# Splitting the channel product of an attention and spectral-mixing kernel into two products made under the weight stream, with a tail of four matmuls per tile

## The chip, the cores and the metric

The kernel runs on one core of one Trainium2 chip. The metric is device time in microseconds (us) of one launch. Three runs of the kernel before took 563.3, 560.01 and 556.01 us, median 560.01 us. The profile is of one further execution, which took 558.66 us; the span between its first and its last instruction is 556.9 us.

A core has a matrix engine (PE, with its weight loads shown apart as PEld), a vector engine (DVE), a scalar engine (ACT), a general engine (POOL) and a sync engine (SP). POOL, SP and ACT can issue DMA copies, which all run on the core's same 16 DMA engines. Products land in PSUM; DVE and ACT move them to SBUF.

## The reference

```python
scores = scale * np.matmul(q, k.transpose(0, 1, 3, 2))     # 8 batches, 8 heads, 576 positions, 64 wide
mask = (rel >= 0) & (rel < 64)                             # causal window of 64
attn = softmax(where(mask, scores, -1e9))
x = heads of matmul(attn, v) joined                        # (8, 576, 512)

X = np.fft.rfft(x, axis=1)                                 # 64 lowest modes are mixed
Yr = einsum('bmd,mde->bme', Xr, w_r) - einsum('bmd,mde->bme', Xi, w_i)
Yi = einsum('bmd,mde->bme', Xr, w_i) + einsum('bmd,mde->bme', Xi, w_r)
y = np.fft.irfft(Y, n=S, axis=1)
u = x + y
out = u + np.maximum(u @ w_ch, 0.0)
```

The mode weights `w_r` and `w_i` are 64 matrices of 512x512 each in float32: 134 MB to read. The output is 9.44 MB of float32. The channel product is `u @ w_ch`, with one 512x512 matrix for all positions.

## The kernel before, in words

**Weights.** POOL's queue carries the weights: 256 copies of 256 KB (as written; each reads 512 KB of float32 and casts to bf16), one per mode, half of the input channels, and real or imaginary part (`load_weights`, L94 to L106). A tile is 128 partitions by 1024 elements. The first 8 tiles go to the pool `wave`, the others to `ring` with 25 buffers, and after the attention to a second ring of 24 more. POOL issues in order, each copy waits on its engine's queue until its buffer is free, and until the copy eight places earlier has landed (eight semaphores are shared in turn).

**Attention.** A hand-written software pipeline (L379 to L410) runs over 40 units of heads and positions. It leaves the attention output `x_sb` in bf16 and its forward transform `XQ` for both channel halves. After half of the units it also runs ten early steps (`early_step`): one per group of four modes, with the first channel half; their sums wait in `Yacc`.

**The stream.** Then 22 late steps follow (L441 to L448). `mode_step` does 16 matmuls on eight weight tiles: 32 output rows per mode, four modes side by side in the array. Groups 10 to 15 take two steps each (both halves), then groups 0 to 9 one each. `finish_group` moves a finished group from PSUM to the SBUF tile `stg` on DVE (L425 or L427) and issues eight copies of 8 KB from SP's queue (L430, L431). Each takes 8 rows of `stg` (one per batch, 1 KB each) to one partition of `Yall`, where the mode stands on the partition and the batch in the row:

```python
nc.sync.dma_start(out=late["Yall"][m:m + 1, :, :], in_=stg[r0:r0 + B, :])
```

**The seam.** When the stream is done, the table `trigI` of the inverse transform is made (L454 to L474: an iota on POOL, then DVE, a sine on ACT, then DVE). DVE has the last three `stg` behind this in its order.

**The tail.** For each of 40 tiles (8 batches, 4 tiles of 128 positions and one of 64) PE does one matmul for the inverse transform (L488), DVE adds `x_sb` (L491), PE transposes the sum in float32 four times (L494), ACT or DVE moves that to SBUF (L498), PE does four matmuls with `wch` (L501), DVE takes the maximum with zero and adds (L505), and SP issues the store (L507).

The order within each engine is as written inside `manual_schedule`; the seam and the tail stand outside of it and are interleaved by the planner.

Of the kernel before, what the change touches and what calls it, by code (L numbers as in the profile page):

```python
# [17 lines left out]
RING = 25  # L18
# [7 lines left out]
def kernel(  # L26
# [40 lines left out]
    mask_t = consts.tile([128, 3, 4, 128], BF16, name="mask_t")  # L67
    trigF = consts.tile([128, NTC, 2 * NM], BF16, name="trigF")
    trigI = consts.tile([2 * NM, S], BF16, name="trigI")
# [9 lines left out]

    ring = pool("ring", bufs=RING, side="right")  # L80
    wave = pool("wave", bufs=FIRST, side="right")
# [3 lines left out]
    order = [(p, 0) for p in range(4 * EARLY)]  # L85
    for grp in range(EARLY, NGRP):
        order += [(4 * grp + i, hb) for hb in range(2) for i in range(4)]
    for grp in range(EARLY):
        order += [(p, 1) for p in range(4 * grp, 4 * grp + 4)]
    wlist = [(p, hb, ri) for p, hb in order for ri in range(2)]  # L90
    wtiles = {}
    nload = 0

    def load_weights(n):  # L94
        nonlocal nload
        for _ in range(n):
            if nload == len(wlist):
                return
            p, hb, ri = wlist[nload]
            w = (wave if nload < FIRST else ring).tile(  # L100
                [128, NJ, DM], BF16, name="wi" if ri else "wr", tag="wt")
            src = moe_w_i if ri else moe_w_r
            nc.gpsimd.dma_start(  # L103
                out=w, in_=src[p, HALF * hb:HALF * hb + HALF, :].rearrange("(p j) e -> p j e", j=NJ))
            wtiles[p, hb, ri] = w
            nload += 1  # L106


    def mode_step(psm, pairs, hb, first, last):
# [10 lines left out]
        for p in pairs:  # L120
            for ri in range(2):
                wtiles.pop((p, hb, ri))

    with tc.manual_schedule():
        ps_mm = pool("ps_mm", space=PSUM)
        rawp = pool("rawp", bufs=2)
# [191 lines left out]
        zero_xq(0, nc.vector)  # L318

# [40 lines left out]
        def early_step():  # L360
            nonlocal step, post
            grp = step
            late["psm"] = ps_mm.tile([128, DM], FP32, name="psm")
            psm = late["psm"]
            mode_step(psm, range(4 * grp, 4 * grp + 4), 0, first=True, last=True)
            load_weights(8 if step >= FIRST // 8 else 0)
            if step == FIRST // 8 - 1:
                close(wave)
                post = pool("post", side="right", reuse_waits="tile")
                XQ[1] = post.tile([128, NJ, NM + 1, 3, B], BF16, name="XQ1")  # L370
                zero_xq(1, nc.gpsimd)
                late["Yacc"] = post.tile([128, EARLY, DM], FP32, name="Yacc")
                late["Yall"] = post.tile([2 * NM, B, DM], BF16, name="Yall")
            nc.scalar.copy(out=late["Yacc"][:, grp, :], in_=psm)
            step += 1

        post = None

        for it in range(-3, NU + 3):  # L379
# [24 lines left out]
            if 0 <= it < NA:  # L404
                load_weights((it + 1) * (FIRST + RING) // NA - nload)
# [3 lines left out]
            if it >= NA and (it - NA) % 2 == 0 and step < EARLY:  # L409
                early_step()  # L410
        do_dft(NG - 1)
# [3 lines left out]
        close(smp, ptp, pp, ps_m, ps_pv, ps_pt, ps_s, vdp, vfp, qtp, rawp, ps_mm)  # L415

        ring2 = pool("ring2", bufs=24, reuse_waits="tile")
        stgpool = pool("stgpool", bufs=3, reuse_waits="tile")
        ps_mc = pool("ps_mc", bufs=3, space=PSUM, reuse_waits="tile")
        nc.gpsimd.dma_start(out=wch, in_=moe_w_ch.rearrange("(c p) e -> p c e", p=128))  # L420

        def finish_group(grp, psm):
            stg = stgpool.tile([128, DM], BF16, name="stg")
            if grp < EARLY:
                nc.vector.tensor_tensor(out=stg, in0=psm, in1=late["Yacc"][:, grp, :], op=ALU.add)  # L425
            else:
                nc.vector.tensor_copy(out=stg, in_=psm)  # L427
            for g in range(4):
                m, r0 = 4 * grp + g, 32 * g
                nc.sync.dma_start(out=late["Yall"][m:m + 1, :, :], in_=stg[r0:r0 + B, :])  # L430
                nc.sync.dma_start(out=late["Yall"][NM + m:NM + m + 1, :, :], in_=stg[r0 + B:r0 + 2 * B, :])  # L431

        ring_, ring = ring, ring2
        load_weights(24)
        late_steps = []
        for grp in range(EARLY, NGRP):
            late_steps += [(grp, 0, True, False), (grp, 1, False, True)]
        for grp in range(EARLY):
            late_steps.append((grp, 1, True, True))
        psm = None  # L440
        for grp, hb, f, l in late_steps:  # L441
            if f:
                psm = ps_mc.tile([128, DM], FP32, name="psm")
            mode_step(psm, range(4 * grp, 4 * grp + 4), hb, f, l)
            ring = ring_ if nload % 16 < 8 else ring2
            load_weights(8)
            if l:
                finish_group(grp, psm)  # L448

    close(ps_mc, stgpool, ring2)  # L450

    with ExitStack() as p15:
        stmp2 = p15.enter_context(tc.tile_pool(name="stmp2", bufs=1))
        MtI = stmp2.tile([128, S], FP32, name="MtI")  # L454
        nc.gpsimd.iota(MtI, pattern=[[1, S]], base=0, channel_multiplier=0,
                       allow_small_or_imprecise_dtypes=True)
        nc.vector.tensor_scalar(out=MtI, in0=MtI, scalar1=Mcol, scalar2=None, op0=ALU.mult)
        Gph = stmp2.tile([128, 1], FP32, name="Gph")
        nc.vector.tensor_scalar(out=Gph, in0=Gcol, scalar1=0.25, scalar2=0.25, op0=ALU.mult, op1=ALU.add)
        Qi = stmp2.tile([128, S], FP32, name="Qi")  # L460
        Ri = stmp2.tile([128, S], FP32, name="Ri")
        nc.vector.tensor_scalar(out=Qi, in0=MtI, scalar1=1.0 / S, scalar2=Gph, op0=ALU.mult, op1=ALU.add)
# [77 lines left out]
```

## Time and profile before

| what | value |
|---|---|
| median of three runs | 560.01 us |
| profiled execution, its span | 558.66 us, 556.9 us |
| PE busy, PEld busy, DVE busy, ACT busy | 323.2, 181.5, 188.0, 137.3 us |
| last weight matmuls begin | 454.65 us into the span |
| first matmul of the tail | 481.32 us |
| last store's DVE instruction begins | 553.01 us |
| weight copies, median issue to landing | 9.7 and 9.8 us |
| bytes moved by POOL's queue | 77.63 MB as written |

The page divides the span into 40 slices and gives each engine's busy tenths, the clock granted to PE in tenths, and the busy share of the DMA engines. The chain is the sequence of work that ended last, followed back from the end. A timeline row gives start, duration, engine, line, operation, tiles and count, and in brackets how long the engine was idle before it and what ended that. A DMA answer gives packets by size and by queue, in the window asked for; q0 is POOL's queue, q1 the queues of SP and ACT. The share beside a queue is the time of its packets over 16 engines.

### The profile page before, as it was taken

What the parts mean: (1) busy time and instruction counts of PE and PEld (TensorE: products, weight loads), DVE (VectorE), ACT (ScalarE), POOL (GpSimd) and SP (SyncE); (2) the same over time, 40 slices, a digit from 0 to 9 for tenths busy, and PEclk for the clock granted to TensorE, in tenths of its full rate; (3) what the DMA queues carried; (4) which work ended last, traced back from release to release, by engine and by line L of the source; (5) the groups of instructions that cost most, each with busy time, mean ns of one, the idle gap of its engine ahead of it and who ended that gap; (6) DMA issues with size and microseconds to landing.
All of it is one profiled execution on the core that took longest, in us unless ns stands there. A gap on an engine that the chain in (4) does not pass through costs nothing.

```text
span 556.9 us, 9561 instructions
## 1 busy us (share of the span) xinstructions
PE 323.2 (58%) x3868; PEld 181.5 (33%) x3896; DVE 188.0 (34%) x329; ACT 137.3 (25%) x216; POOL 217.9 (39%) x356
## 2 busy tenths in 40 slices
PE   0598889797884696442343343433433420499996
PEld 0466666665653463100000000000000000266664
DVE  6267366465560364000000000000000022288885
ACT  0455564656651545100000000000000001022221
POOL 7184574654743636443444344344344400000000
PEclk9999696789995889655555555555555555599999
DMA  9799999999899998999999999999999940034343
GB/s 156 117 160 192 193 203 199 181 163 184 144 206 203 203 208 158 209 209 247 210 210 211 211 209 211 210 211 211 211 205 211 210 87 8 8 141 138 136 136 130
DMA packets 95676, 98.17 MB, mean 176 GB/s; under 512 B 47504, under 2 KB 57744, under 8 KB 95632
## 3 DMA queue, kind: packets, MB, share of 16 engines
q0 software_dynamic: 50192, 77.63, 77.4%
q1 hardware_dynamic: 45440, 19.93, 15.5%
q8 instruction: 30, 0.49, 0.3%
q14 instruction: 14, 0.11, 0.1%
HBM read 163.58 MB, written 9.44 MB: 311 GB/s over the span
## 4 chain that ended last, share of the span: by engine, by line
DMA 49%; PE 28%; ACT 7%; issue 5%; SPq 4%; DVE 4%; POOL 2%; POOLq 0%; DVEq 0%; ACTq 0%
DMA wi<-in_moe_w_i_dram 33%; DMA vf<-in_v_dram 9%; DMA wr<-in_moe_w_r_dram 7%; PE pout L501 7%; PE tr L169 3%; PE psut L494 3%; PE s L219 3%; PE pt L227 2%; PE psy L488 2%; ACT XQ L270 2%; PE s L193 2%; PE s L204 2%; ACT p L221 2%; PE px L268 1%; SPq L151 1%
## 5 line engine op out<-in xcount | busy, mean ns | idle before, releaser
L115 PE MATMUL psm<-wr,XQ 128*32 128x512 bf16 x256 | 68.9, 545 | 142.5 <-DMA wr<-in_moe_w_r_dram 141.9
L103 POOL DMA_DIRECT2D wi<-in_moe_w_i_dram x128 | 68.8, 538 | 78.6 <-DMA wi<-in_moe_w_i_dram 60.2
L103 POOL DMA_DIRECT2D wr<-in_moe_w_r_dram x128 | 68.8, 538 | 76.5 <-DMA wr<-in_moe_w_r_dram 67.4
L115 PEld LDWEIGHTS <-XQ 128*32 128x32 bf16 x512 | 19.3, 104 | 220.9 <-issue 204.0
L211 DVE TENSOR_REDUCE mx<-s 128x4 fp32r<-128x512 f32 x72 | 49.8, 691 | 75.1 <-PE s L201 64.1
L469 ACT ACT_TABLE_LOAD x1 | 1.3, 1283 | 230.0 <-DVE Qi L467 230.0
L427 DVE CAST stg<-psm 128x512 bf16<-128x512 f32 x6 | 4.1, 691 | 130.1 <-PE psm L115 130.1
L115 PE MATMUL psm<-wi,XQ 128*32 128x512 bf16 x256 | 43.8, 557 | 6.5 <-DMA wi<-in_moe_w_i_dram 6.5
L501 PE MATMUL pout<-wch,utt 128*128 128x512 f32 (+1 forms) x160 | 43.6, 410 | 0.5 <-ACT utt L498 0.5
L221 ACT ACTIVATE p<-s 128x512 bf16<-128x512 f32 x72 | 40.2, 606 | 9.4 <-PE s L219 8.4
L498 ACT CAST utt<-psut 128x512 fp32r<-128x512 f32 (+1 forms) x33 | 19.1, 579 | 70.3 <-PE psut L494 70.3
L169 PE MATMUL tr<-ident_bf,rawk 72*64 72x72 bf16 x512 | 17.5, 219 | 31.4 <-DMA rawk<-in_k_dram 21.1
L491 DVE TENSOR_TENSOR ut<-x_sb,psy 128x512 f32<-128x512 bf16 (+1 forms) x40 | 27.1, 683 | 18.7 <-PE psy L488 17.2
L505 DVE SCALAR_TENSOR_TENSOR ot<-pout,ut 128x512 f32<-128x512 f32 (+1 forms) x40 | 27.5, 687 | 14.4 <-PE pout L501 14.4
L230 DVE COPY pts<-pt 128x1024 bf16<-128x1024 bf16 (+1 forms) x40 | 25.3, 633 | 19.0 <-PE pt L227 19.0
L172 ACT COPY kT<-tr 128x576 bf16<-128x576 bf16 x32 | 20.4, 638 | 44.1 <-PE tr L169 44.1
L219 PE MATMUL s<-mx,ident_r 128*128 128x512 f32 x72 | 30.6, 497 | 0.1
L425 DVE TENSOR_TENSOR stg<-psm,Yacc 128x512 bf16<-128x512 f32 x10 | 6.7, 689 | 68.4 <-PE psm L115 39.5
L501 PEld LDWEIGHTS pout<-wch,utt 128*128 128x128 f32 (+1 forms) x160 | 26.3, 177 | 10.5 <-ACT utt L498 3.2
L204 PE MATMUL s<-kT,qT 64*64 64x64 bf16 x320 | 26.5, 212 | 4.9 <-issue 4.9
L258 DVE TENSOR_TENSOR x_sb<-o,r 128x512 bf16<-128x512 f32 (+1 forms) x40 | 27.6, 690 | 1.4
L488 PE MATMUL psy<-Yall,trigI 128*128 128x512 bf16 (+1 forms) x34 | 12.3, 401 | 26.0 <-DMA Yall<-stg 25.7
(85 smaller groups left out, 510.4 us busy)
## 6 DMA issues: line engine op xcount, KB each, us to landing
wr<-in_moe_w_r_dram POOLq DMA_DIRECT2D x128, 256.0 KB, 9.7
wi<-in_moe_w_i_dram POOLq DMA_DIRECT2D x128, 256.0 KB, 9.8
vf<-in_v_dram SPq DMA_DIRECT2D x64, 128.0 KB
out_dram<-ot SPq DMA_DIRECT2D x32, 256.0 KB
rawk<-in_k_dram POOLq DMA_DIRECT2D x16, 288.0 KB, 7.9
rawq<-in_q_dram POOLq DMA_DIRECT2D x16, 288.0 KB, 8.6
Yall<-stg SPq DMA_DIRECT2D x128, 8.0 KB
vf<-in_v_dram SPq DMA_DIRECT2D x16, 64.0 KB
```

The source lines that it names most:

```text
L103: nc.gpsimd.dma_start(out=w, in_=src[p, HALF * hb:HALF * hb + HALF, :].rearrange("(p j) e -> p j e", j=NJ))
L115: nc.tensor.matmul(out=psm[32 * g:32 * g + 32, :], lhsT=XQ[hb][:, j].rearrange("k m t b -> k (m t b)")[:, (3 * p + 1 - ri) * B:(3 * p + 5 ...
L169: nc.tensor.transpose(out=pt[64 * hh:64 * hh + 64, j, :], in_=raw[:, 2 * pr + hh, j, :], identity=ident_bf[0:72, 0:72])
L204: nc.tensor.matmul(out=s[ro, t, 0:64], lhsT=lq, rhs=kT[ro, 64 * n:64 * n + 64], start=False, stop=True, skip_group_check=True)
L211: nc.vector.tensor_reduce(out=mx, in_=s, axis=AX.X, op=ALU.max, negate=True)
L219: nc.tensor.matmul(out=s, lhsT=ident_r, rhs=mx.unsqueeze(2).to_broadcast([128, 4, 128]), start=False, stop=True, skip_group_check=True)
L221: nc.scalar.activation(out=p[:, 4 * c2:4 * c2 + 4, :], in_=s, func=ACT_F.Exp, scale=EX_SCALE)
L230: nc.vector.tensor_copy(out=ps[:, 0:nt, :], in_=pt[:, 0:nt, :])
L258: nc.vector.tensor_tensor(out=xo.rearrange("p c (h d) -> p c h d", d=64), in0=ov[:, :, :, 0:64], in1=rb, op=ALU.mult)
L491: nc.vector.tensor_tensor(out=ut[:nt, :], in0=x_sb[:nt, b, tch, :], in1=psy[:nt, :], op=ALU.add)
L501: nc.tensor.matmul(out=pout[:nt, :], lhsT=utt[:, ech * nt:(ech + 1) * nt], rhs=wch[:, ech, :], start=(ech == 0), stop=(ech == NDCH - 1))
L505: nc.vector.scalar_tensor_tensor(out=ot[:nt, :], in0=pout[:nt, :], scalar=0.0, in1=ut[:nt, :], op0=ALU.max, op1=ALU.add)
```

## The change

`u @ w_ch` becomes `x @ w_ch` plus `y @ w_ch`, and the second is the inverse transform of `Y @ w_ch`. Both new factors are made during the stream:

- `x_product` makes `XW`, 40 tiles of `x @ w_ch`, two after each late step (sixteen in the first eight of the first ten steps, two after each of the last twelve). `finish_group` also makes `Z = Y @ w_ch` for the group's four modes. Both use `channel_product`: four bf16 transposes on PE, a copy on ACT, four float32 matmuls on PE.
- The result of a group goes to `Yall` in four copies of 16 KB instead of eight of 8 KB, and to `Zall` (float32) in four copies of 32 KB. Each takes 16 rows of the staging tile to two partitions; mode rows are now interleaved (real, imaginary). All are issued by SP, except the last group's `Zall` copies, which ACT issues.
- The inverse tables (`trigI`, and a float32 one, `trigIr`) are made before the first late step. Their iota stands in POOL's queue behind the loads of the early steps.
- The tail has four matmuls per tile: identity times `x_sb` and the inverse transform of `Yall` into one bank, identity times `XW` and the inverse transform of `Zall` into another; then a copy on ACT, a maximum and sum on DVE and the store.
- The weight tiles of a step come real parts first, then imaginary (before: alternating). The order of steps is groups 0 to 9 (second half), then 10 to 15. The rings are 11 and 14 buffers and no second ring of 24; once the weights of the first ten late steps are in, only the ring of 11 is used, and `XW` takes the other's place. `wch` is loaded after the sixth early step rather than after the attention.

```diff
-    ring = pool("ring", bufs=RING, side="right")
+    ringA = pool("ringA", bufs=NRA, side="right", reuse_waits="tile")
+    ringB = pool("ringB", bufs=NRB, side="right", reuse_waits="tile")
...
+    steps = [(grp, 0) for grp in range(EARLY)] + [(grp, 1) for grp in range(EARLY)]
+    steps += [(grp, hb) for grp in range(EARLY, NGRP) for hb in range(2)]
+    wlist = [(p, hb, ri) for grp, hb in steps for ri in range(2) for p in range(4 * grp, 4 * grp + 4)]
...
+        def channel_product(src, n):
+            pt = ps_t.tile([128, NDCH, 128], BF16, name="ptr")
+            for c in range(NDCH):
+                nc.tensor.transpose(out=pt[:, c, 0:n], in_=src[0:n, 128 * c:128 * c + 128],
+                                    identity=ident_bf[0:n, 0:n])
+            tr = trpool.tile([128, NDCH, 128], FP32R, name="tr")
+            nc.scalar.copy(out=tr[:, :, 0:n], in_=pt[:, :, 0:n])
+            pz = ps_z.tile([128, DM], FP32, name="pz")
+            for c in range(NDCH):
+                nc.tensor.matmul(out=pz[0:n, :], lhsT=tr[:, c, 0:n], rhs=wch[:, c, :],
+                                 start=(c == 0), stop=(c == NDCH - 1))
+            return pz
...
         def finish_group(grp, psm):
...
-            for g in range(4):
-                m, r0 = 4 * grp + g, 32 * g
-                nc.sync.dma_start(out=late["Yall"][m:m + 1, :, :], in_=stg[r0:r0 + B, :])
-                nc.sync.dma_start(out=late["Yall"][NM + m:NM + m + 1, :, :], in_=stg[r0 + B:r0 + 2 * B, :])
+            pz = channel_product(stg, 128)
+            zst = stgpool.tile([128, DM], FP32R, name="zst")
+            nc.vector.tensor_copy(out=zst, in_=pz)
+            last = grp == NGRP - 1
+            for t, rows, eng in ((Yall, stg, nc.sync),
+                                 (Zall.bitcast(FP32), zst.bitcast(FP32), nc.scalar if last else nc.sync)):
+                for g in range(4):
+                    m2, r0 = 2 * (4 * grp + g), 32 * g
+                    eng.dma_start(out=t[m2:m2 + 2, :, :], in_=rows[r0:r0 + 2 * B, :])
...
+        def x_product(n):
+            for _ in range(n):
...
+                pz = channel_product(x_sb[:, b, c, :], rows[i])
+                xw = late["xp"].tile([128, DM], FP32R, name=f"xw{i}")
+                nc.vector.tensor_copy(out=xw[0:rows[i]], in_=pz[0:rows[i]])
+                XW[i] = xw
...
+        inverse_tables()
...
+        for i, (grp, hb) in enumerate(steps[EARLY:]):
...
+            mode_step(psm, range(4 * grp, 4 * grp + 4), hb, f, hb == 1)
+            load_weights(len(wlist))
+            if hb == 1:
+                finish_group(grp, psm)
+            if i < EARLY:
+                x_product(min(2, NX0 - len(XW)))
+            else:
...
+                x_product(2)
...
+        for i, (b, c) in enumerate(tiles):
...
+            nc.tensor.matmul(out=psu[:nt, :], lhsT=ident_bf[:nt, :nt], rhs=x_sb[:nt, b, c, :], start=True, stop=False)
+            nc.tensor.matmul(out=psu[:nt, :], lhsT=trigI[:, ts_], rhs=Yall[:, b, :], start=False, stop=True)
...
+            nc.tensor.matmul(out=pso[:nt, :], lhsT=ident_r[:nt, :nt], rhs=XW[i][:nt, :], start=True, stop=False)
+            nc.tensor.matmul(out=pso[:nt, :], lhsT=trigIr[:, ts_], rhs=Zall[:, b, :], start=False, stop=True)
+            ut = ringA.tile([128, DM], FP32, name="ut", tag="wt")
+            nc.scalar.copy(out=ut[:nt, :], in_=psu[:nt, :])
+            nc.vector.scalar_tensor_tensor(out=ut[:nt, :], in0=pso[:nt, :], scalar=0.0,
+                                           in1=ut[:nt, :], op0=ALU.max, op1=ALU.add)
+            nc.sync.dma_start(out=out[b, 128 * c:128 * c + nt, :], in_=ut[:nt, :])
```

## The prediction

> **What bounds the kernel now.** I read the slices of the page first, then the chain of waits, the timeline around the end of the weights, and the DMA answers for three windows. The slices, four of their rows:
>
> ```profile
> PE   0598889797884696442343343433433420499996
> ...
> DVE  6267366465560364000000000000000022288885
> ...
> PEclk9999696789995889655555555555555555599999
> DMA  9799999999899998999999999999999940034343
> ```
>
> A slice is 13.9 us. From slice 17 to 32 the DMA engines are full, PE is busy 4 tenths at half clock and DVE does nothing: the late steps wait for weights. Then come two slices in which nothing is busy (the seam), then the tail, where PE is full. The last late steps, the seam and the tail, from the timeline and the chain:
>
> ```profile
> 246.31 1.01 PE L115 MATMUL psm<-wi,XQ 128*32 128x512 bf16 x5 [0.27 <-DMA wi<-in_moe_w_i_dram]
> 256.32 1.01 PE L115 MATMUL psm<-wi,XQ 128*32 128x512 bf16 x5 [0.27 <-DMA wi<-in_moe_w_i_dram]
> 268.87 1.01 PE L115 MATMUL psm<-wi,XQ 128*32 128x512 bf16 x5 [0.17 <-DMA wi<-in_moe_w_i_dram]
> 278.89 1.01 PE L115 MATMUL psm<-wi,XQ 128*32 128x512 bf16 x5 [0.17 <-DMA wi<-in_moe_w_i_dram]
> ...
> 434.60 1.01 PE L115 MATMUL psm<-wi,XQ 128*32 128x512 bf16 x5 [0.31 <-DMA wi<-in_moe_w_i_dram]
> 444.63 1.01 PE L115 MATMUL psm<-wi,XQ 128*32 128x512 bf16 x5 [0.19 <-DMA wi<-in_moe_w_i_dram]
> ```
>
> ```profile
> 463.42 0.69 DVE stg L425
> ...
> 479.27 1.92 DMA Yall<-stg
> 481.32 0.58 PE psy L488
> ...
> 553.01 0.68 DVE ot L505
> ```
>
> A step of eight tiles takes 10.02 us where nothing else moves (246.31 to 256.32, 434.60 to 444.63), 1.25 us per tile. The one step with `wch` in it takes 12.55 us: 1 MB, 32 rows of 2 KB on each of 16 engines, cost 2.53 us, 79 ns per row. So other bytes are not free: they lengthen the stream. From 278.89 to 434.60 there are 15 steps, 150.3 us at 10.02, but 155.7 pass: 5.4 us for the 11 groups whose `Yall` copies fall in it, 0.49 us per group. The DMA answers, first for 456 to 482 us (only `Yall` copies), then for 485 to 556 us (only stores):
>
> ```profile
> DMA packets 385, 0.21 MB, mean 8 GB/s; under 512 B 192, under 2 KB 384, under 8 KB 384
> q1 hardware_dynamic: 384, 0.20, 3.7%
> ```
>
> ```profile
> DMA packets 5252, 9.49 MB, mean 134 GB/s; under 512 B 640, under 2 KB 640, under 8 KB 5248
> q1 hardware_dynamic: 5248, 9.44, 38.4%
> ```
>
> 40 stores leave 640 tiny packets, 16 each: one end mark per DMA engine. 24 `Yall` copies leave 192, 8 each: a copy of 8 rows runs on 8 engines, a row (1 KB) and a mark on each. Engine time: 3.7% of 16 x 26 us over 192 pairs is 80 ns for row and mark; 38.4% of 16 x 71 us over 4608 rows and 640 marks is 91 ns per 2 KB row if a mark is 25 ns (estimate; at 0 to 40 ns the row is 95 to 89). And 0.49 us per group over eight copies is 61 ns per pair: the eight engines were the same in all eight copies (spread evenly over 16 it would be 4 pairs, 122 ns each, more than their 80), and the tile of weights waits for its slowest engine.
>
> **Part 1, the seam.** Before: last weight matmuls end at 455.27 (454.65 + 0.62), the tail starts at 481.32. Gone are 7 us of tables and 24 copies at 0.68 us each. What takes their place, in a chain at half clock: `stg` on DVE 0.9 (0.69 and the hand-over); four transposes 0.7 (eight bf16 ones take 0.97 at full clock, L227); ACT 0.7 (0.59); four products 1.9 (1.00 at full clock, L501); `zst` 0.8; four `Zall` copies on ACT at SP's 0.68, 2.7. Behind these in ACT's queue stand the copies of the last two `x_product`, on which PE waits before the tail: 0.6, then products 1.5, transposes 0.6, copy 0.7, products 1.5. Sum 12.6 us. The last `Zall` copy lands 1.92 us after its issue (the chain's row for `Yall`), at about 9, so it is hidden by these; were they gone it would end the seam there.
>
> **Part 2, the tail.** Before: 8.67 us per five tiles (chain, 510.96 to 519.63), bound by PE. After: four matmuls of 512 columns per tile. L501 gives 0.25 us each (x4 in 1.00), the bf16 L488 0.22 to 0.30; 40 x 4 x 0.25 = 40.0, and 1.5 for the clock, which was 0.50 in the first 3 us of the tail and 0.91 in the next. Beside it, hidden: ACT 40 x 0.59 = 23.6, DVE 40 x 0.69 = 27.6, stores 4608 rows / 16 x 91 ns = 26 us. After PE's last matmul 0.2 to DVE's start and 3.9 from there to the end (553.01 to 556.9): 4.1.
>
> Without any effect on the stream the span would be 455.27 + 12.6 + 41.5 + 4.1 = 513.5, a gain of 43.4 us.
>
> **Part 3, what PE now does under the stream.** A step with `finish_group` and two `x_product` costs PE at full clock 1.1 (16 matmuls, chain at 142.42) + 0.9 + 3 x (0.5 + 0.7 + 1.0 + 0.1) = 8.9 us, at half clock 1.9 + 0.9 + 3 x 3.3 = 12.7. The weights need 10.02, so this is hidden at full clock only, or if the stream is slower. Which clock? Cut into windows of 3.4 us, the attention shows 0.50 after windows in which PE was idle (167 to 174) and 1.00 after one full window (177 to 181); products with gaps of 0.7 us lie between, nearer to the second. Eleven buffers are 13.8 us of weights; PE's longest absence from them is 0.9 + 3 x 3.3 = 10.8 and the reload about 2: just enough, cost nothing.
>
> **Part 4, the tables.** The iota stands behind the load of tile 104 in POOL's order. In before that place (the `wch` issue) is reached at 248.98; 2.5 us later now, as `wch` comes earlier. Tables and sine took 7.1 us (455.7 to 462.8), `trigIr` adds 0.5; DVE's first `stg` waits behind them, to about 259.5, and PE behind that, since about 240. 25 buffers cover 31 us: cost 0 to 2 us, and PE is two steps behind for a while.
>
> **Part 5, the result copies.** Per group now 64 rows of 1 KB and 64 of 2 KB in eight copies, each from 16 partitions to 2. How many engines carry one, no row shows: before both sides counted 8. [...] Bounds. On 16 engines: one row per copy and engine, 4 x (55 + 25) + 4 x (91 + 25) = 0.78 us of engine time, times 61/80 to 0.9 for what overlaps: 0.6 to 0.7 per group. On 2 engines, the target's outer count: eight rows each, 4 x (8 x 55 + 25) + 4 x (8 x 91 + 25) = 4.9 us, at 61/80 3.7; I take 4.3. [...] 15 of the 16 groups finish inside the stream: 15 x 4.3 = 64.5, less the 5.4 of before: +59 us. A step with a group then takes 14.3 us, which covers the 8.9 to 12.7 of part 3, and part 4.
>
> [...]
>
> **Sum.** 513.5 + 59 = 572.5 of span; the execution's own time was 1.8 above its span: 574 us. The profiled 558.66 lies 1.4 under the median of 560.01. With 3.7 to 4.9 per group 565 to 583, and 5 us for seam and tail: 560 to 586 for this case. 2% (11.2 us, 571.2) is about what can be told from no change here.
>
> **Rivals.**
> 1. *The copies spread over 16 engines* (ends faster). 15 x 0.65 - 5.4 = +4.4, and 2 for the tables: 513.5 + 6.4 + 1.8 = 522. The point from which it decides: the gain of 43.4 is used up at (43.4 + 5.4) / 15 = 3.25 us per group, so with three engines or more (2.9) the kernel is not slower. For it: 16 rows are there to be spread. [...]
> 2. *PE becomes the bound*, spread copies and half clock: 12.7 against 10.3 in eight steps (+19), and per pair of the last twelve 2 x 1.9 + 0.9 + 5 x 3.3 = 21.2 against 20.6 (+4): 522 + 23 = 545. Against it: PE busy over 60% had full clock in the attention.
> 3. *Hot engines and a late PE together*: with two engines the weights arrive late and PE, cold, holds the eleven buffers: six pairs at 3 us more, 574 + 18 = 592.
>
> **Chances.** Forecast case 0.70, rival 1 0.18, rival 2 0.05, rival 3 0.07. Of the forecast case some 0.62 lies over 571.2: slower 0.50, within 2% 0.26, faster 0.24. The range reaches down into rival 1 so that no more than 2 in 10 is left out: 520 to 586.
>
> **What would show it.** Steps of about 14 us in the first ten late steps and 12 on average in the rest, with some 160 GB/s where 211 stood (eight tiles and a group's copies, 2.3 MB, in 14.3 us) though PE waits for weights: part 5. Two tiny packets per result copy. Steps at 10.4: rival 1. PE without waits for weights: rival 2. Seam of 12 to 13 us, tail of 1.0 us per tile at full clock: parts 1 and 2. I would be wrong above all if the copies use other engines each time.

## The result, and the profile after

The changed kernel takes 577.04 us (median of 4 runs, 575.65 to 577.67), beside 561.25 us for the kernel before on the same chip (median of 4, 556.01 to 563.3). The ratio is 1.0293, with a 95% interval from 1.0216 to 1.0369: slower, by about what was predicted (574 us). The profiled execution has a span of 575.7 us.

From the page of the changed kernel, the rows of slices that were shown of the kernel before, and the rate of transfer. A slice is 14.4 us here:

```profile
PE   0698878879827794217777764357586756756997
...
DVE  6257656466523371032212111011111111111665
...
PEclk9999998699978697555656577556656757565999
DMA  9799999998999999998999999497969898850665
GB/s 156 119 170 194 205 170 161 190 202 139 205 203 203 203 236 204 210 209 161 183 201 164 164 155 157 82 199 141 193 123 202 165 208 151 169 100 14 219 237 202
```

From slice 18 on PE is busy mostly five to seven tenths, at a clock of 5 to 7 tenths, where it was busy three or four before. The DMA row shows nines and eights in most slices, but the row below tells more: 140 to 170 GB/s in many of them, and 82 in slice 25, where the kernel before moved 211 in its undisturbed late steps. The engines look busy and move less. The seam is one slice (14 GB/s, slice 36) instead of two, the tail three instead of six.

Ends of late steps and the end of the stream, from the timeline of the changed kernel (start, duration, engine, line, operation, tiles; in brackets PE's idle time before it and what ended that):

```profile
372.51 1.07 PE L129 MATMUL psm<-wi,XQ 128*32 128x512 bf16 x8
...
387.12 1.01 PE L129 MATMUL psm<-wi,XQ 128*32 128x512 bf16 x5 [1.08 <-DMA wi<-in_moe_w_i_dram]
...
401.63 0.59 PE L129 MATMUL psm<-wi,XQ 128*32 128x512 bf16 x5 [1.30 <-DMA wi<-in_moe_w_i_dram]
...
465.14 1.01 PE L129 MATMUL psm<-wi,XQ 128*32 128x512 bf16 x5 [0.67 <-DMA wi<-in_moe_w_i_dram]
...
489.85 1.01 PE L129 MATMUL psm<-wi,XQ 128*32 128x512 bf16 x5 [0.64 <-DMA wi<-in_moe_w_i_dram]
...
514.38 1.01 PE L129 MATMUL psm<-wi,XQ 128*32 128x512 bf16 x5 [0.64 <-DMA wi<-in_moe_w_i_dram]
```

The first three rows, each a step with a group, come 14.6 and 14.5 us apart where steps came 10.02 apart before, and PE waits for weights in the last two. From 266 to 358 us, behind the stall for the tables, PE works off full buffers instead, without such waits, mostly 11 to 13 us per step. In the last twelve steps, of which every second finishes a group, two steps take 24.5 to 25.0 us (465.14 to 489.85 to 514.38), 12.3 us each. The last weight matmuls end at 515.4 us; in the kernel before this was 455.27. So the stream is 60 us longer, and what follows it is 41 us shorter: 575.7 - 515.4 = 60.3 us, where it was 556.9 - 455.3 = 101.6.

What the DMA engines do while the stream is slow is seen best where POOL, too, has to wait. DMA answer of the changed kernel for 362 to 371 us, in 40 parts of 0.23 us:

```profile
DMA  9897998899995421111111101111111110111111
GB/s 219 155 223 137 150 137 146 164 187 228 187 218 100 82 55 27 27 32 27 23 32 32 41 27 36 36 27 36 36 36 27 27 46 27 36 27 36 36 27 36
```

For 5.5 us one to two tenths of the engines' time are in use (two of sixteen would be 0.125), and about 30 GB/s are moved. By this reading two engines are still working through what is queued on them, and the others have run out. A weight tile leaves 16 end marks with its 128 rows, so by the marks it is split over all sixteen (that makes 144 packets, and from 300 to 390 us POOL's queue moved 6973 for 49 tiles issued, 142 each), and is not there until those two have brought their share: from issue to landing it took 14.0 us in these 90 us (median), where it was 9.7 and 9.8 before. The end marks of the result copies say the same. DMA answer of the changed kernel for 515.6 to 531 us, when only the last group's eight copies run:

```profile
GB/s 0 0 0 0 0 0 0 0 0 0 0 0 0 0 0 11 32 43 11 32 43 43 43 21 32 27 5 29 21 35 16 27 27 16 0 0 0 0 0 0
DMA packets 144, 0.20 MB, mean 13 GB/s; under 512 B 16, under 2 KB 80, under 8 KB 144
...
q10 hardware_dynamic: 72, 0.13, 3.2%
q1 hardware_dynamic: 72, 0.07, 1.5%
```

Sixteen tiny packets for eight copies are two each, and the 64 rows of each kind are there in full (72 = 64 + 8): by the marks a copy of 16 rows to two partitions ran on two engines.

The seam, from the timeline of the changed kernel:

```profile
515.43 0.69 DVE L490 CAST stg<-psm 128x512 bf16<-128x512 f32 x1 [7.67 <-PE psm L129]
...
517.51 2.08 PE L481 MATMUL pz<-wch,tr 128*128 128x512 f32 x4 [0.73 <-ACT tr L478]
...
520.35 3.63 ACTq L499 DMA_DIRECT2D Zall<-zst  x4
524.08 0.58 ACT L478 CAST tr<-ptr 128x512 fp32r<-128x512 bf16 x1 [6.62 <-DMA Zall<-zst]
...
524.82 2.57 SPq L499 DMA_DIRECT2D Yall<-stg  x4
...
529.85 0.63 PE L548 MATMUL psu<-Yall,trigI 128*128 128x512 bf16 x1 [0.24 <-issue]
```

The tail's first matmuls begin at 529.4 (this row is the second of them), 14.0 us after the stream. ACT's four issues of `Zall` took 3.63 us: by the chain the last waited until the copy issued at 520.35 had landed, 2.99 us later. ACT's next copy, with PE behind it, stood in line. SP issued the last `Yall` copies only at 524.8, though `stg` was there at 516.1. The tail then runs at 0.91 us per full tile to the last DVE instruction at 571.87, 42.5 us, and 3.8 us pass to the end.

### The profile page after: what moved, and what is told of

Read it like the earlier page. It is cut to its first block, busy times and chain, and to the rows that moved or that the text cites. A ratio compares the mean times of both kernels' runs of the same rounds, so it can differ in the third digit from the quotient of the medians.

```text
span 575.7 us, 10274 instructions
## 1 busy us (share of the span) xinstructions
PE 389.6 (68%) x4119; PEld 220.6 (38%) x4144; DVE 199.1 (35%) x343; ACT 172.4 (30%) x279; POOL 218.0 (38%) x356
## 4 chain that ended last, share of the span: by engine, by line
DMA 37%; PE 33%; issue 15%; ACT 6%; POOL 3%; DVE 3%; SPq 2%; ACTq 0%; POOLq 0%; DVEq 0%
DMA wr<-in_moe_w_r_dram 21%; PE pz L481 9%; DMA wi<-in_moe_w_i_dram 6%; PE psm L129 3%; DMA vf<-in_v_dram 3%; DMA rawq<-in_q_dram 3%; PE tr L186 3%; ACT tr L478 2%; DMA rawk<-in_k_dram 2%; PE s L236 2%; PE pso L550 2%; PE ptr L475 2%; PE pso L551 2%; PE psu L547 2%; PE psu L548 2%
## 5 line engine op out<-in xcount | busy, mean ns | idle before, releaser
L481 PE MATMUL pz<-wch,tr 128*128 128x512 f32 (+1 forms) x224 | 105.1, 615 | 43.2 <-ACT tr L478 43.2
L478 ACT CAST tr<-ptr 128x512 fp32r<-128x512 bf16 (+1 forms) x56 | 31.1, 555 | 241.5 <-PE ptr L475 234.9
L481 PEld LDWEIGHTS pz<-wch,tr 128*128 128x128 f32 (+1 forms) x224 | 56.3, 280 | 67.2 <-ACT tr L478 56.3
L513 DVE CAST xw<-pz 128x512 fp32r<-128x512 f32 (+1 forms) x40 | 27.5, 689 | 100.2 <-PE pz L481 100.2
L475 PE MATMUL ptr<-ident_bf,stg 128*128 128x128 bf16 x64 | 8.9, 286 | 46.8 <-DVE stg L488 42.1
L129 PE MATMUL psm<-wr,XQ 128*32 128x512 bf16 x256 | 31.3, 531 | 8.9 <-DMA wr<-in_moe_w_r_dram 6.9
L493 DVE CAST zst<-pz 128x512 fp32r<-128x512 f32 x16 | 11.1, 692 | 64.6 <-PE pz L481 39.0
L554 DVE SCALAR_TENSOR_TENSOR ut<-pso,ut 128x512 f32<-128x512 f32 (+1 forms) x40 | 27.6, 690 | 14.6 <-PE pso L551 7.1
L186 PEld LDWEIGHTS <-rawk 72*64 72x64 bf16 x512 | 14.7, 126 | 39.4 <-DMA rawk<-in_k_dram 24.5
L553 ACT COPY ut<-psu 128x512 f32<-128x512 f32 (+1 forms) x40 | 23.4, 584 | 20.7 <-PE psu L548 15.6
```

The source lines that it names most:

```text
L129: nc.tensor.matmul(out=psm[32 * g:32 * g + 32, :], lhsT=XQ[hb][:, j].rearrange("k m t b -> k (m t b)")[:, (3 * p + 1 - ri) * B:(3 * p + 5 ...
L186: nc.tensor.transpose(out=pt[64 * hh:64 * hh + 64, j, :], in_=raw[:, 2 * pr + hh, j, :], identity=ident_bf[0:72, 0:72])
L478: nc.scalar.copy(out=tr[:, :, 0:n], in_=pt[:, :, 0:n])
L481: nc.tensor.matmul(out=pz[0:n, :], lhsT=tr[:, c, 0:n], rhs=wch[:, c, :], start=(c == 0), stop=(c == NDCH - 1))
L513: nc.vector.tensor_copy(out=xw[0:rows[i]], in_=pz[0:rows[i]])
L554: nc.vector.scalar_tensor_tensor(out=ut[:nt, :], in0=pso[:nt, :], scalar=0.0, in1=ut[:nt, :], op0=ALU.max, op1=ALU.add)
```

## The experiments

Two theories were set against each other. The first is the prediction's: the result copies run on two DMA engines, and the stream goes at the pace of these two. The second is that of rivals 2 and 3: PE, at half clock and with three products per step, holds the weight buffers, and the eleven buffers at the end add to it. The ratios are to the kernel before on the same chip. The runs come from several chips, so that medians in us compare less closely than ratios; the ends of the stream are from one profile each. Overview:

| kernel | median, us | ratio to before (95%) | last weight matmuls end, us |
|---|---|---|---|
| changed kernel | 577.04 | 1.0293 (1.0216 to 1.0369) | 515.4 |
| rows8 | 551.62 | 0.9914 (0.9874 to 0.9954) | 486.7 |
| nocopies | 530.88 (one run) | | 468.7 |
| noxw | 579.91 (one run) | | 517.5 |
| zall2 | 625.11 (one run) | | 557.9 |
| before2p | 564.29 | 1.0059 (1.0015 to 1.0104) | 466.4 |
| rows8_iota | 539.55 | 0.9673 (0.9593 to 0.9752) | 471.6 |
| rows8_zb | 545.59 | 0.9763 (0.9695 to 0.9832) | 477.7 |
| zlate | 520.84 | 0.9323 (0.9247 to 0.9398) | 454.3 |
| after_iota | 576.84 | 1.0287 (1.0156 to 1.0417) | 513.0 |
| nocopies_iota | 521.29 | 0.9315 (0.9236 to 0.9394) | 460.0 |
| rows8_pipe | 542.2 | 0.9632 (0.9517 to 0.9748) | 471.7 |

### One partition per copy, so eight engines (rows8)

```diff
-                    m2, r0 = 2 * (4 * grp + g), 32 * g
-                    eng.dma_start(out=t[m2:m2 + 2, :, :], in_=rows[r0:r0 + 2 * B, :])
+                    for ri in range(2):
+                        m, r0 = 2 * (4 * grp + g) + ri, 32 * g + B * ri
+                        eng.dma_start(out=t[m:m + 1, :, :], in_=rows[r0:r0 + B, :])
```

> The changed kernel with one edit: each result copy takes 8 rows of the staging tile to one partition, as in the kernel before, so 8 copies for Yall and 8 for Zall per group instead of 4 and 4. Theory 1 (two DMA engines carry the result copies and set the pace of the stream): 8 engines now carry them, 8 x (55 + 25) + 8 x (91 + 25) = 1.6 us of engine time per group, about 1.3 of lengthening instead of 4.3; 45 us less for the weights alone, but PE at half clock would then bind in part of the stream, so 23 to 45 us less than the 577: 532 to 554 us. End marks 8 per copy. Theory 2 (PE at half clock and the eleven buffers set the pace, the copies do not matter): 577 plus 3 for the eight Zall copies on ACT at the end, 574 to 583.

551.62 us, ratio 0.9914: the same bytes, in twice the copies, and 25 us less by the medians, 21 by the ratios. The stream ends 29 us sooner. On ACT's queue (q10) the last group's eight `Zall` copies leave 128 packets, 64 rows and eight marks each. That speaks for the two engines. But 486.7 is still 37 us above 449.9, where the stream of the kernel before would have ended without its result copies (455.27 - 5.4; called the floor from here on), and the seam got longer: with twice the copies to issue, the tail's first matmul with `Yall` waits until 507.3, 20.6 us after the stream instead of 14.5.

### No result copies (nocopies)

```diff
-                for g in range(4):
+                for g in range(4 if last else 0):
```

> The changed kernel without the result copies of all groups but the last (Yall and Zall are zeroed by DVE once instead, 5 to 10 us of DVE ahead of the first group; so the mixing of 60 modes is missing from the output). Theory 1: the stream has no copies to wait for; its floor by DMA is 454.65 - 5.4 = 449, by PE at half clock some 490: 505 to 555 us in all. Theory 2: no change, 570 to 580.

530.88 us. The product of each group is still made. Without its copies the stream is 47 us shorter. It is not at the floor, though: the page of this run shows where.

```profile
PE   0599798697983869540176676677577677748996
...
GB/s 151 132 148 195 187 199 130 200 210 201 148 204 203 205 200 223 235 210 209 194 53 167 208 209 210 210 209 205 191 184 206 170 206 172 192 63 62 225 247 189
```

PE stands still in slices 18 and 19, waiting for the tables and for the zeroing of `Yall` and `Zall`, which here stands before the first `stg` in DVE's order: 26.1 us, where the changed kernel has 19.7. When all buffers are full the stream stops (53 and 167 GB/s, slices 20 and 21), and after slice 27 it falls below 210 several times.

### PE's work halved (noxw)

```diff
-                pz = channel_product(x_sb[:, b, c, :], rows[i])
-                xw = late["xp"].tile([128, DM], FP32R, name=f"xw{i}")
-                nc.vector.tensor_copy(out=xw[0:rows[i]], in_=pz[0:rows[i]])
-                XW[i] = xw
+                if i == 0:
+                    xw = late["xp"].tile([128, DM], FP32R, name="xw0")
+                    nc.vector.tensor_copy(out=xw, in_=x_sb[:, 0, 0, :])
+                XW[i] = xw if i == 0 else XW[0]
```

> The changed kernel without the forty x products (one constant tile stands in for all of XW, so that term is missing from the output); result copies, Z products and the tail's four matmuls stay. Theory 1: the stream ends where it did, at 510 to 517, as the two engines still carry the copies; the seam is 3 to 6 us shorter as no x products stand behind the last copies: 569 to 576. Theory 2: PE has 80 fewer of its 165 us in the stream, which then runs at 10 to 10.5 us per step: 520 to 540.

579.91 us: 40 products less on PE, and nothing gained. (It is 4 us above the range that the first theory gave: the stream ends 2 us later, and the 3 to 6 us that were to be saved behind it are not, 60.6 us instead of 60.3.) The stretch in which the eleven buffers are all there is goes no faster either. Ends of steps from the timeline of this run:

```profile
442.95 1.01 PE L129 MATMUL psm<-wi,XQ 128*32 128x512 bf16 x5 [0.65 <-DMA wi<-in_moe_w_i_dram]
...
467.48 1.01 PE L129 MATMUL psm<-wi,XQ 128*32 128x512 bf16 x5 [0.65 <-DMA wi<-in_moe_w_i_dram]
...
492.01 1.01 PE L129 MATMUL psm<-wi,XQ 128*32 128x512 bf16 x5 [0.65 <-DMA wi<-in_moe_w_i_dram]
```

Two steps take 24.5 us here and 24.5 to 25.0 in the changed kernel, although from 400 to 515 us POOL waits only 20.6 us for buffers that PE's weight matmuls hold, against 47.8 in the changed kernel. This ends the second theory for the changed kernel. Here the two engines can be seen to set the pace. The chain of waits of this run, start and duration:

```profile
268.23 14.62 DMA Yall<-stg
282.86 0.02 issue
282.87 14.58 DMA Yall<-stg
297.46 0.02 issue
297.47 14.60 DMA Yall<-stg
312.07 0.02 issue
312.09 14.61 DMA Yall<-stg
```

The chain passes from one group's `Yall` copies to the next, 14.6 us each. Eight weight tiles took 10.02 us before, which leaves 4.6 us of the two engines for a group's copies (estimate, 14.6 - 10.02).

### Twice the Zall copies (zall2)

```diff
-                for g in range(4):
+                for g in list(range(4)) * (2 if t is not Yall and not last else 1):
```

> The changed kernel with every Zall copy but the last group's issued twice (same data, same place). Theory 1: 15 groups x 2.3 to 3.0 us more on the two engines, +35 to +45 us: 612 to 622, or more where SP's queue of copies holds up the staging tiles. Theory 2: 577 to 582.

625.11 us, 48 us more and 3 above the range; the stream ends 42.5 us later. Over 15 groups that is 2.8 us per set of `Zall` copies: 32 rows of 2 KB and four marks on each of the two engines, 89 ns per row (estimate). More rows on the pair, and the stream ended later.

### The copies' form in the kernel before (before2p)

```diff
-                m, r0 = 4 * grp + g, 32 * g
-                nc.sync.dma_start(out=late["Yall"][m:m + 1, :, :], in_=stg[r0:r0 + B, :])
-                nc.sync.dma_start(out=late["Yall"][NM + m:NM + m + 1, :, :], in_=stg[r0 + B:r0 + 2 * B, :])
+                m2, r0 = 2 * (4 * grp + g), 32 * g
+                nc.sync.dma_start(out=late["Yall"][m2:m2 + 2, :, :], in_=stg[r0:r0 + 2 * B, :])
```

> The kernel before with one edit: a group goes to Yall in four copies of 16 rows to two partitions instead of eight of 8 rows to one (mode rows interleaved, the table's formulas to match). No channel product under the stream, PE has much room. Hot pair: 32 rows of 1 KB on each of two engines, 1.4 to 1.9 us per group against 0.49, so the 13 groups inside the stream cost 12 to 18 us more; the seam, where SP issues 12 copies instead of 24 at 0.68 us, gets 8 us shorter: ratio to the kernel before 1.005 to 1.02, last weights 466 to 473 us into the span. Rival (the form of the copies costs nothing, PE and buffers are what made the changed kernel slow): last weights at 455 or sooner, 8 us gained, ratio 0.985.

Ratio 1.0059 (1.0015 to 1.0104). The last weight matmuls start at 465.37 instead of 454.65, 10.7 us later, a little under the range; the seam is 8 us shorter, as expected (the tail begins at 484.05, 17.7 us after the stream instead of 26). One part of the change alone, in a kernel whose PE has much room, brings its price. The 12 copies of its last three groups leave 24 marks, two each. Per group 10.7 / 13 + 0.49 = 1.3 us for 32 rows of 1 KB on each engine, 41 ns per row (estimate). With `Zall`'s 2.8 that is 4.1 us per group, by two kernels that share neither the work nor the pace.

### The tables' wait taken away (after_iota, rows8_iota, nocopies_iota)

In all three the iota is issued at the start of the kernel, into a tile that stays, so that DVE's tables and the first late step no longer wait behind POOL's loads:

```diff
+    MtI = post.tile([128, S], FP32, name="MtI")
...
+        nc.gpsimd.iota(MtI, pattern=[[1, S]], base=0, channel_multiplier=0,
+                       allow_small_or_imprecise_dtypes=True)
         load_qk(1)
...
         def inverse_tables():
-            MtI = stmp2.tile([128, S], FP32, name="MtI")
-            nc.gpsimd.iota(MtI, pattern=[[1, S]], base=0, channel_multiplier=0,
-                           allow_small_or_imprecise_dtypes=True)
```

> rows8 with the iota of the inverse tables issued at the start, so that DVE's tables and the first late step's hand-over don't wait for the loads of the early steps. If PE's stall of 20 us at the start of the late steps is covered by the 25 full buffers (prediction, part 4: 0 to 2 us): within 2 us of rows8, 550 to 553. If it costs, because a PE at half clock can't catch up with a stream that only loads on 8 engines: 535 to 546, with the stall gone.

539.55 us, ratio 0.9673 against rows8's 0.9914: 13 us. The stall was not free there; the miss is of the prediction's own estimate. In the trace of rows8 the rate falls to 132 GB/s from 264 to 272 us and to 68 from 352 to 360, where the loads change over to the ring of eleven and POOL waits 11.0 us for PE to release a buffer; rows8_iota moves 187 in the second stretch.

> The changed kernel with the iota of the inverse tables issued at the start, so that the first late step doesn't wait for the tables. Hot pair theory: the stream is paced by the two engines of the result copies; the stall costs only the stretch in which the 25 buffers were all full (264 to 272 us, where the DMA share fell to 0.70): 3 us less, up to 5: ratio to the kernel before 1.02 to 1.03. Rival (the late PE is what costs, as in rows8, where the same edit gave 12 us): 564 to 567, ratio 1.00 to 1.01.

576.84 us, ratio 1.0287 against 1.0293: nothing that can be told, with an interval of some 7 us either way, and the rival's 1.00 to 1.01 lies outside it. The stream ends 2.4 us sooner in the one profile. The same 20 us of PE's time that cost 13 us in rows8 cost little or nothing in the changed kernel, since there the pair of engines sets the pace and PE catches up. Its steps now show the pace of the pair from the beginning. Timeline of after_iota:

```profile
257.75 1.01 PE L130 MATMUL psm<-wi,XQ 128*32 128x512 bf16 x5 [1.23 <-DMA wi<-in_moe_w_i_dram]
...
272.39 0.59 PE L130 MATMUL psm<-wi,XQ 128*32 128x512 bf16 x5 [1.08 <-DMA wi<-in_moe_w_i_dram]
...
286.99 0.59 PE L130 MATMUL psm<-wi,XQ 128*32 128x512 bf16 x5 [1.29 <-DMA wi<-in_moe_w_i_dram]
...
301.63 1.01 PE L130 MATMUL psm<-wi,XQ 128*32 128x512 bf16 x5 [1.08 <-DMA wi<-in_moe_w_i_dram]
...
316.25 0.59 PE L130 MATMUL psm<-wi,XQ 128*32 128x512 bf16 x5 [1.08 <-DMA wi<-in_moe_w_i_dram]
```

Five ends of steps 14.6 us apart, each with a wait for weights: 14.3 had been predicted. The same steps in rows8_iota, with eight engines:

```profile
258.20 1.04 PE L130 MATMUL psm<-wr,XQ 128*32 128x512 bf16 x8
259.03 1.07 PE L130 MATMUL psm<-wi,XQ 128*32 128x512 bf16 x8
269.19 1.04 PE L130 MATMUL psm<-wr,XQ 128*32 128x512 bf16 x8
270.02 0.77 PE L130 MATMUL psm<-wi,XQ 128*32 128x512 bf16 x8
280.53 1.04 PE L130 MATMUL psm<-wr,XQ 128*32 128x512 bf16 x8
281.36 1.07 PE L130 MATMUL psm<-wi,XQ 128*32 128x512 bf16 x8
```

Steps of 11.2 us without any wait for weights: PE goes at its own pace here, with three products at a granted clock of 0.58. Yet the DMA engines are nearly full as well (206 GB/s from 245 to 335 us, 211 undisturbed before); rows8_pipe below tells the two limits apart. Rival 2's bound is close by once the copies are spread.

> nocopies with the early iota: result copies of all groups but the last are left out (Yall and Zall are zero there), and the first late step doesn't wait for the tables. If the 16 us by which nocopies stayed above the DMA floor (531 against 515) are the stall followed by a PE at half clock that can't catch up: 517 to 522. If they are the steps of a half-clock PE as such, from the first step on (12.7 against 10 us): 527 to 532.

521.29 us, 10 less than nocopies. The stream ends at 460.0 instead of 468.7: about half of the 18.8 us that nocopies kept above the floor was the stall, there lengthened by the zeroing.

### Smaller rows for Zall (rows8_zb)

```diff
-        Zall = zpool.tile([2 * NM, B, DM], FP32R, name="Zall")
+        Zall = zpool.tile([2 * NM, B, DM], BF16, name="Zall")
...
-            zst = stgpool.tile([128, DM], FP32R, name="zst")
+            zst = stgpool.tile([128, DM], BF16, name="zst")
...
-            nc.tensor.matmul(out=pso[:nt, :], lhsT=trigIr[:, ts_], rhs=Zall[:, b, :], start=False, stop=True)
+            nc.tensor.matmul(out=pso[:nt, :], lhsT=trigI[:, ts_], rhs=Zall[:, b, :], start=False, stop=True)
```

> rows8 with Zall and its staging tile in bf16 (1 KB rows instead of 2 KB; the inverse transform of Z uses the bf16 table). Eight engines then spend about 0.5 us less per group on Zall: 15 x 0.45 = 7 us less in the stream if the result copies still set its pace: 543 to 547. If PE with its products (12.7 us per step at half clock) and the eleven buffers set the pace in rows8: within 3 us of it, 549 to 554.

545.59 us, ratio 0.9763 against 0.9914; the intervals don't meet, and the stream ends 9 us sooner. So on eight engines, too, the bytes of the copies counted here.

### The products of a step overlapped (rows8_pipe)

The edit to rows8_iota, cut to its core; `channel_product` is split at the copy on ACT, and a step without a result does the same with its two tiles of `x`:

```diff
-            pz = channel_product(stg, 128)
+            x_trans(nx)
+            ztr = transposed(stg, 128)
+            x_prod()
+            pz = product(ztr, 128)
```

> rows8_iota with the channel products of a step overlapped: the transposes of all its tiles first, then the products, so that PE doesn't wait 0.7 us for ACT between them. At half clock a step then needs PE for 1.9 + 3 x 0.65 + 3 x 2.07 = 10.1 us instead of 12.7, near the stream's 10 to 11.4; if the denser work brings the full clock, some 6. So PE no longer sets the pace: 526 to 534 (the last group's Z is made last, which lengthens the seam by 2 to 4). If the copies on eight engines, not PE, hold rows8_iota at 540: 538 to 544.

542.2 us, ratio 0.9632 against 0.9673, and the intervals overlap: no gain that can be told. (The four runs took 535.14 to 543.76 us; the profile is of the one of 543.54.) PE did become free, but the next limit stood right behind. From the answer of the windows for 245 to 335 us (length, then busy time of each engine, granted clock, DMA share, GB/s), first rows8_iota, then rows8_pipe:

```profile
245.00:335.00 90.00, 67.61 (x317) 33.43 (x316) 21.41 (x31) 12.25 (x22) 33.39 (x63) 0.58 1.13 206
```

```profile
245.00:335.00 90.00, 60.76 (x315) 32.24 (x314) 21.69 (x32) 11.71 (x22) 33.71 (x64) 0.80 1.13 207
```

The granted clock went from 0.58 to 0.80 with the same products, and PE now waits for weights in each step, yet the bytes per second are the same and so is the end of the stream (471.7 against 471.6). The first matmuls on imaginary weights of its steps lie at 245.85 and, nine steps later, at 347.75: 11.3 us per step, 1.3 over the 10.02. With 15 x 1.3 us over the floor of 449.9 the stream would end at 469.4, by this estimate, so the copies on eight engines alone account for nearly all of it: both limits lay at the same place. The expected 526 to 534 was wrong, since it took PE's pace for the only one.

### A version that beats both (zlate)

`Yall` goes in the form of the kernel before (eight copies, eight engines; the last group's from SP and ACT). `Zall` isn't copied: after the stream, Z is made from `Yall`, one product per batch, one batch ahead of the tail, and DVE puts it straight into place, since mode rows already stand on the partitions.

```diff
         def finish_group(grp, psm):
...
-            pz = channel_product(stg, 128)
-            zst = stgpool.tile([128, DM], FP32R, name="zst")
-            nc.vector.tensor_copy(out=zst, in_=pz)
...
+        nc.vector.tensor_copy(out=Zall[:, 0, :], in_=channel_product(Yall[:, 0, :], 128))
         for i, (b, c) in enumerate(tiles):
...
+            if b + 1 < B and c == 0:
+                ztr = transposed(Yall[:, b + 1, :], 128)
+            if b + 1 < B and c == 2:
+                nc.vector.tensor_copy(out=Zall[:, b + 1, :], in_=product(ztr, 128))
```

> Candidate: Yall in copies of 8 rows to one partition as in the kernel before, no Zall copies and no Y w product in the stream; Z is made after the stream, one product per batch in the tail (Yall of the batch transposed, four matmuls, DVE to Zall, one batch ahead). x products stay under the stream. Stream: floor 449 to 455 plus 7 for Yall (last weights at 455 to 466, PE needs 8.5 us of a step even at half clock); seam 10 to 12; tail 42.5 plus 8 x 1.5 = 54; end 4: span 523 to 536, time 525 to 538. If PE's late start or the clock still hold the stream, 540 to 550.

520.84 us, ratio 0.9323 (0.9247 to 0.9398): 39 us less than the kernel before, some 54 less than the changed one by the ratios, and 4 under the range. Answer of the windows of this run for 300 to 450 us:

```profile
300.00:450.00 150.00, 107.98 (x429) 43.60 (x428) 23.13 (x34) 14.18 (x26) 59.51 (x112) 0.53 1.11 207
```

PE is busy 72% of the time at a clock of 0.53, and the stream runs at 207 GB/s and ends at 454.3: two products per step fit, even at half clock and with the stall for the tables. Then 12.8 us of seam and 50 us of tail with eight products in it.

## Why the prediction was right, step by step

The range of 520 to 586 us would have held rival 1 too, so the time alone decides nothing about the mechanism; the marks and the runs do.

**Part 5, the result copies: right in kind, and in size partly by luck.** That it would be two was the author's estimate: no row of the kernel before shows it, and no run shows what sets the number. The marks show two for 16 rows to two partitions (changed kernel, before2p) and eight for 8 rows to one (before, rows8). That a mark takes 25 of the 80 ns was an estimate as well; no answer shows a mark alone. The 4.3 us per group stands against 4.6 (noxw, pace 14.6 - 10.02), 4.1 (zall2 and before2p added up) and, over the whole stream, 515.4 - 449.9 = 65.5 us for 15 groups, 4.4 each. So +59 us was predicted and 60.1 came. rows8, nocopies and zall2 show it by taking the engines' load away, or adding to it: between no copies, those of the change, and these with `Zall` twice, the end of the stream goes from 468.7 over 515.4 to 557.9. The luck is in the 4.3, which was taken between 3.7 and 4.9 without a reason. The last group's copies, which ran with no stream beside them, took 1.5% and 3.2% of 16 x 15.4 us, so a group keeps each of the two engines busy for some 5.8 us (estimate), not 4.9: the 2 KB rows were priced too low, 123 ns each with their share of the marks where 94 was taken. Of this the stream lost three quarters, 4.4 of 5.8, close to the prediction's 61/80. And the pace of 10.02 us, said to hold where nothing else moves, was read at 246.31 to 256.32 too, where SP issued a group's eight `Yall` copies (248.1 to 253.8); 434.60 to 444.63, with no copies issued, bears it out.

**Rival 1, sixteen engines at 522, did not happen;** that a step of 14.3 covers what PE does was also right: noxw and after_iota left the time as it was.

**Part 3, PE under the stream: the clock was wrong, and its harmlessness right only through part 5.** Full clock was taken as nearer; the granted clock was 0.53 to 0.68 in the windows from 240 to 465 us. That PE had full clock in the attention when busy over 60% was a wrong reading: in the kernel before it was busy for 6.46 of 7 us at 0.56 from 62 to 69 us, for 6.09 at 0.50 from 83 to 90, and for all 3.40 us at 0.50 from 177.4 to 180.8. "Eleven buffers cost nothing" fails as well when the cover is gone: in nocopies_iota POOL waits 55 us for `psm` to release buffers, and the stream ends at 460.0, 10 us above the floor, without any result copies. In the changed kernel this is hidden by the pair of engines, as noxw shows. The prediction said that cover would be lost only in rivals 2 and 3, and gave them 12%; it should have counted on either clock, and said that the kernel stands on two limits close together.

**Part 4, the tables: right in the cost, the reason only in part.** First `stg` at about 259.5 was predicted; it came somewhat sooner, at 255.9, and PE stood still for 19.7 us. Cost 0 to 2 us predicted; after_iota gains 0.3 us by the ratios, less than can be told, and 2.4 in the end of the stream. The reason given, that 25 buffers cover it, was not the whole one. Behind the stall PE does the step's three products before it takes the next weights, and POOL ran out of buffers. Its timeline in the changed kernel:

```profile
257.70 0.53 POOL L116 DMA_DIRECT2D wr<-in_moe_w_r_dram  x1 [0.68 <-PE ptr L475]
267.70 1.59 POOL L116 DMA_DIRECT2D wr<-in_moe_w_r_dram  x3 [9.47 <-PE psm L129]
```

From 264 to 272 us the rate fell to 129 GB/s. In rows8, with the same buffers and the same 19.7 us, the stall cost 13 us. It is nearly free in the changed kernel because the pair sets a pace at which PE can catch up.

**Part 1, the seam: 14.0 instead of 12.6.** The chain was the one named. The mis-sized terms are the four issues on ACT, 3.63 us instead of 2.7, because the last waits for an earlier one to land, and the products: 2.08 us instead of 1.9, and the two behind it 2.1 and 2.0 instead of 1.5 each. That the last `Yall` copies would be issued so late, at 524.8, was not foreseen. It was nearly the end of the seam. The profile puts SP's wait before them, 23.3 us, down to a `Zall` copy; nothing moved from 515.6 to 521.4 us, so it was none of an earlier group still under way. Why they had to wait for ACT's copies no run shows. In nocopies, where SP had issued none before, they went out at 469.5, right behind `stg`. **Part 2, the tail: 42.5 instead of 41.5**, at 0.91 us per full tile, and 3.8 instead of 4.1 at the end.

The sum: stream +1.1, seam +1.4, tail +1.0, end -0.3 make the 3.2 us by which the span of 575.7 stands over the 572.5 predicted.

The other side of the sum, "513.5 without any effect on the stream", was too good by some 10 us. nocopies_iota, which has neither copies nor stall, took 521.3; by the prediction's terms it would have been 513.5 - 5.4 + 1.8 = 510. It cost nothing here because the copies' price swallowed PE's; that this error did not show in the time is luck too.

## What to carry to other kernels

Before a small copy is put beside a stream that fills the DMA engines, count its end marks: here they were 16 for a weight tile or a store, eight for a copy of 8 rows to one partition and two for one of 16 rows to two. What the stream lost was about three quarters of the time of the rows on one of these engines (4.4 of 5.8 us per group, estimate). Fewer and larger copies can be dearer to a stream than many small ones: in before2p half the copies, twice as large, made it end 10.7 us later. A stall or a slow engine that costs nothing is free only under the present limit: with the copies spread, the stall for the tables, PE's clock and the copies on eight engines came up one after the other, so the next limit has to be priced before the gain is counted.

## What was not expected of the hardware

- In these runs neither PE's busy share nor the gaps between its products told the granted clock. With gaps of 0.7 us between transposes and products rows8_iota had 0.58 from 245 to 335 us (PE busy for 67.6 of 90 us); with the gaps closed rows8_pipe had 0.80 (60.8 us). But rows8, with the gaps, had 1.00 from 300 to 330 us, busy for 18.5 of 30, and made a step in 8.2 to 8.5 us. So closing the gaps is not shown to be what raised the clock. (One profile of each.) From the timeline of rows8:

```profile
302.37 0.60 PE L129 MATMUL psm<-wi,XQ 128*32 128x512 bf16 x8
...
310.56 0.60 PE L129 MATMUL psm<-wi,XQ 128*32 128x512 bf16 x8
...
319.06 0.60 PE L129 MATMUL psm<-wi,XQ 128*32 128x512 bf16 x8
```

- The two engines alone moved about 30 GB/s (23 to 46 from 365.4 to 371 us of the changed kernel). A row of 1 KB on each of them cost the stream 41 ns (before2p), a row of 2 KB 89 ns (zall2), marks included; with no stream beside them the last group's rows took 58 and 123 ns (estimates from the 1.5% and 3.2% above). The pair of 1 KB row and mark on eight engines had cost 61 ns before.
- SP's queue waited for the landing of its own slow copies in 63 places between 240 and 515 us of the changed kernel (34 times for `Zall`, 42.7 us in all, and 29 times for `Yall`, 28.0 us). The copies' slowness on two engines thus reached DVE too, through the two staging tiles: in the changed kernel DVE waited 25.6 us for `zst` to be copied away, and 10.7 for `stg`.
